# Attention and a SwiGLU block on one Trainium2 core: batch 3's keys turned by transposing transfers, K and V loaded in spread blocks, Q in halves

## The chip, the cores and the metric

The kernel runs on one core of a Trainium2 chip. The core has TensorE (PE, the matmuls; PEld is its weight load), VectorE (DVE), ScalarE (ACT), GpSimd (POOL) and SyncE (SP), each with an instruction queue of its own that is worked off in order, and 16 DMA engines that serve transfers issued from SP, ACT and POOL. The metric is the device time of one execution in microseconds, as a median over runs. Lower is better.

## The reference

Eight batches of causal attention with a learned decay, eight heads of 64, 576 positions, then an RMS norm and a SwiGLU feed-forward over all 4608 tokens. Everything is float32 in HBM.

```python
B, H, S, D = 8, 8, 576, 64
cum    = np.cumsum(np.maximum(s, 0.0), axis=-1)
scores = q @ k.T / 8 + np.minimum(-(cum_q - cum_k), 0.0)     # causal: k <= q
attn   = softmax(scores) @ v                                  # per batch and head
x      = attn as [4608, 512]
xn     = x / sqrt(mean(x * x) + 1e-6) * rms_g
out    = (silu(xn @ w_gate) * (xn @ w_val)) @ w_out           # 512 -> 1536 -> 512
```

Keys further back than the block before a query's own are left out, with a check at the end that what they weigh is negligible.

## The kernel before

**Chunks and slots.** The feed-forward runs over nine chunks of 512 tokens (`ffn`, lines 741 to 781). A chunk is 144 matmuls of 128x512: twelve times four for the gate (L751), twelve times four for the value (L760), and four times twelve for the output (L773). After each group of four the function `step` (L676) is called once. So a chunk has 36 *slots*, and slot 36c belongs to the end of chunk c's predecessor. Attention of the batches to come is laid into these slots: in each slot `step` takes at most one item from each of several lists, and `place` (L712) puts one piece of attention on PE. Nothing of this is decided on the chip: the Python program works through the slots once, with the planner's lags in slots, and writes every engine's instructions in that order. `done` holds the slot in which a piece was placed, and `ready(lag, key)` says whether it lies `lag` slots back. On the chip semaphores keep the data right; a lag only decides how much time lies between a transfer's issue and its reader.

**A batch's way.** Q, K and V of a batch are cut into five blocks of 128 rows (the last has 64).
- Q comes as float32 by one transfer of 1 MB from ACT's queue (`loads`, L486: `load_kq`, then `load_kq_tail`, three slots apart at least), is cast to bfloat16 into `kqn` by POOL in five pieces (`cast_x`), and from batch 2 on is turned into `kqT` by five transposing transfers from SP's queue (`kq_dma`, L170).
- K of batches 0 to 3 (`b < KB`, KB = 4) comes and is cast in the same way, and is turned on PE: four `t_step` (four transposing matmuls each into PSUM, and a copy to `kqT` by ACT, L203) and one `tail_step` (L220, copy L227). `t_seq` is the list of these. K of batches 4 to 7 comes by five casting transfers from POOL's queue straight into `kqn` (`load_k`, L162) and is turned by `kq_dma` as well. The five `load_k` stand at the head of POOL's list `pool_side`, one in each even slot.
- V comes by five casting transfers from POOL's queue (`load_v`, L186), from the list `v_side`, one in each odd slot.
- `s_step` (L278) makes the scores of a block of keys and half of the heads; ACT makes exponentials of them (L302) out of one PSUM buffer `psS`, POOL masks them (L311), and five slots or more later `av_step` (L344, L350) multiplies by V. Then come the norm (ACT L366, POOL L379 and L382, DVE L389) and `xt_dma` (L394), a transposing transfer from SP that writes `xnT`, which the chunk reads.

`can_s` (L619) decides when scores may stand: for batch 2 and on, five slots after the transfer of Q's block and the one after it, and for `b >= KB` five slots after K's block too. SP's queue holds, in the order of the slots, `kq_dma`, `xt_dma` and the stores of the output.

`free(w)` in `casts` (L519) lets a batch's half of `kqn` be written once the batch two before has been checked by DVE (`check_mag`, L420) and turned. `phase()` is the slot within the chunk.

Of the kernel before, what the change touches and what calls it, by code (L numbers as in the profile page):

```python
# [26 lines left out]
def kernel(  # L27
# [12 lines left out]
    nc = tc.nc  # L40
# [40 lines left out]
    kqTn = kqT.rearrange("d a w (h n) -> d a w h n", h=HP)  # L81
    kqTx = kqT.rearrange("d a w (c h n) -> d a w c h n", c=NSC, h=HP)
    XB = 2
    KB = 4
    v_sb = mp.tile([128, 2, NSC, H, NV], BF16, name="v_sb")

    NE = 8
# [39 lines left out]
    def load_kq(eng, b, w, h0=0, h1=H):  # L127
        src = k if w == 0 else q
        eng.dma_start(
            out=kq32[:, w, h0:h1, 0:256],  # L130
            in_=src[b, h0:h1, 0:512, :].rearrange("h (p r) d -> p h (r d)", r=4))
# [299 lines left out]

    SLOTS = 36
    K2 = 34
    slot = [0]
    first, chunk = [0], [0]
    done = {}
    last = {"S": -9, "AV": -9, "T": -9, "X": -9, "AVT": -9, "L": -9}
    s_seq = [(b, kb, g) for b in range(B) for kb in range(NSC) for g in (0, 1) if kb < 4 or g == 0]
    s_seq.sort(key=lambda x: (1, 0, x[2], x[1]) if x[0] == 1 and x[1] < 2 else (x[0], x[1], x[2], 0))
    av_seq = [(b, qb, g) for b in range(B) for qb in range(NSC) for g in (0, 1)]  # L440
# [3 lines left out]
    t_seq.sort(key=lambda x: (x[0], 9, 0, 0) if x[1] == "tail" else  # L444
               (x[0], x[1] // 2, x[2], x[1]) if x[0] == 1 else (x[0], x[2], x[1], 0))
    pending = []
    pool_side, dve_side, v_side, act_side = [], [], [], []
    x_seq = []

    def at(*key):  # L450
# [2 lines left out]
    def ready(lag, *key):  # L453
        return at(*key) + lag <= slot[0]
# [30 lines left out]

    def loads(b, w, when, lag):  # L486

        def main():
            load_kq(nc.scalar, b, w)
            last["L"] = slot[0]  # L490

        def tail():
            load_kq_tail(nc.scalar, b, w)
            done["raw", b, w] = last["L"] = slot[0]
        n = len(act_side)
        when(act_side, lag, [main, tail])
        act_side[n:] = [(lambda c=c: c() and slot[0] - last["L"] >= 3, f) for c, f in act_side[n:]]

    def casts(b):

        def key(c):
            load_k(b, c)
            done["K", b, c] = slot[0]
            if c == NSC - 1:
                check(b)

        def over(w):
            done["cast", b, w] = slot[0]  # L510
            if b + 1 < B and (w == 1 or b + 1 < KB):
                loads(b + 1, w, early, 4)
            if w == 1:
                x_seq.extend((b, ww, c) for c in range(NSC) for ww in ((1, 0) if b >= KB else (1,)))
            else:
                done["cast", b] = slot[0]
                check(b)

        def free(w):  # L519
            return ready(0, "check", b - 2, w) and (  # L520
                ready(0, "T", b - 2) if w == 0 and b < KB + 2 else
                b < XB + 2 or ready(4, "X", b - 2, w, 4))
        if b >= KB:
            pool_side.extend((lambda: free(0) and slot[0] % 2 == 0, lambda c=c: key(c)) for c in range(NSC))
        fns = [(1, lambda r=r: cast_x(nc.gpsimd, b, 1, r)) for r in range(NSC)]
        if b == 2:
            fns[-1] = (1, lambda: (cast_x(nc.gpsimd, b, 1, NSC - 1), over(1)))
        else:
            fns += [(1, lambda: over(1))]
        if b < KB:  # L530
            fns += [(0, lambda r=r: cast(nc.gpsimd, b, 0, r, r + 1)) for r in range(NSC)]
            fns += [(0, lambda: over(0))]
        if b == 2:

            def put2(queue, *fs):
                queue.extend((lambda: slot[0] >= K2 and free(0) and free(1), f) for f in fs)
            put2(act_side, *[lambda r=r: cast_x(nc.scalar, b, 1, r) for r in (3, 4)],
                 *[lambda r=r: cast(nc.scalar, b, 0, r, r + 1) for r in (0, 1, 2)])
            put2(pool_side, *[lambda r=r: cast_x(nc.gpsimd, b, 1, r) for r in (0, 1)],
                 lambda: (cast_x(nc.gpsimd, b, 1, 2), over(1)),  # L540
                 lambda: cast(nc.gpsimd, b, 0, 3, 4), lambda: (cast(nc.gpsimd, b, 0, 4, 5), over(0)))
            return
        pool_side.extend((lambda w=w: ready(7, "raw", b, w) and free(w), f) for w, f in fns)
# [5 lines left out]
    def after_av(b):  # L549
        if b + 2 < B:  # L550
            if b == 0:
                v_side.extend((lambda: chunk[0] == 1, f) for f in (
                    lambda: (load_v(2, 0), load_v(2, 1)), lambda: (load_v(2, 2), load_v(2, 3)),
                    lambda: (load_v(2, 4), done.__setitem__(("V", 2), slot[0]))))
                return
            early(v_side, 6, [lambda r=r: load_v(b + 2, r) for r in range(NSC)]
                  + [lambda: done.__setitem__(("V", b + 2), slot[0])])

    def do_t(key, **kw):
        b, hp, w = key  # L560
# [58 lines left out]
    def can_s():  # L619
# [6 lines left out]
        if slot[0] - last["S"] < (4 if slot[0] < due - 24 else 3 if slot[0] < due else 2):  # L626
            return False
        if b >= XB:
            return all(ready(5, "X", b, 1, c) for c in (kb, min(kb + 1, 4))) and (
                ready(5, "X", b, 0, kb) if b >= KB else ready(3, "T", b) if kb >= 3 else  # L630
                all(ready(3, "T", b, hp, 0) for hp in (2 * g, 2 * g + 1)))
        if kb >= 3 and not ready(3, "T", b):
            return False
# [4 lines left out]
    def can_av(clear=False):  # L638
# [4 lines left out]
            return False  # L643
        if b > 0 and g == 1 and slot[0] - last["T"] < 3 and not clear:
            return False
        if b > 1 and not ready(8, "V", b):
            return False
        if qb > 0 and not ready(5, "S", b, qb - 1, g):
            return False
# [26 lines left out]
    def step(bare=False):  # L676
# [28 lines left out]
        if slot[0] % 2 and not bare and not (chunk[0] == 0 and phase() >= 24):  # L705
            run_side(v_side)
        if not bare:
            run_side(pool_side)
        place()
        run_side(dve_side)  # L710
# [525 lines left out]
```

## Time and profile before

| | |
|---|---|
| device time, three runs | 363.77, 365.58, 370.51 us; median 365.58 |
| profiled execution: device time | 364.69 us |
| its span | 363.0 us |
| granted TensorE clock | 0.999 |
| feed-forward matmuls L751, L760, L773 | 432 of each, 111.1, 111.1 and 102.5 us busy |
| scores L278, AV L344 and L350 | 320, 256 and 320 matmuls |
| exponentials L302 on ACT | 328, 107.0 us busy |
| transposing transfers | 50 for `kqT`, 36 for `xnT` |
| bytes read from HBM, written | 37.90 MB, 9.44 MB |

Chunk 0's first matmul (L751) begins at 26.8 us, chunk 8's last (L773) at 356.5. The attention of batch 0 stands ahead of chunk 0; batch 3's lies in chunks 1 to 3, batch 7's scores end in chunk 6. A row of groups has line, engine, operation, tiles and shapes, count, then busy time, mean nanoseconds of one, the idle time before it and what ended that. A row of waits has who waited, for whom, the total in us, the number of times and the longest.

### The profile page before, as it was taken

What the parts mean: (1) busy time and instruction counts of PE and PEld (TensorE: products, weight loads), DVE (VectorE), ACT (ScalarE), POOL (GpSimd) and SP (SyncE); (2) the same over time, 40 slices, a digit from 0 to 9 for tenths busy, and PEclk for the clock granted to TensorE, in tenths of its full rate; (3) what the DMA queues carried; (4) which work ended last, traced back from release to release, by engine and by line L of the source; (5) the groups of instructions that cost most, each with busy time, mean ns of one, the idle gap of its engine ahead of it and who ended that gap; (6) DMA issues with size and microseconds to landing.
All of it is one profiled execution on the core that took longest, in us unless ns stands there. A gap on an engine that the chain in (4) does not pass through costs nothing. (4 is left out here: it accounts for less than half of the span.)

```text
span 363.0 us, 6976 instructions
## 1 busy us (share of the span) xinstructions
PE 348.8 (96%) x2383; PEld 160.5 (44%) x2383; DVE 273.4 (75%) x523; ACT 239.8 (66%) x619; POOL 178.2 (49%) x283
## 2 busy tenths in 40 slices
PE   4989999999999999999999999999999999999993
PEld 2445444444445444444444444444444444444441
DVE  6697988698888889788998988884588548827820
ACT  3988884768886778877778768776777653223311
POOL 7959765858865566869737954622232200000000
PEclk9999999999999999999999999999999999999999
DMA  7999999999969399969979994973201130020011
GB/s 228 132 229 256 177 170 259 182 201 193 212 127 138 59 198 138 167 147 163 164 202 124 140 142 105 115 85 90 78 14 17 51 103 1 0 88 29 1 60 60
DMA packets 124096, 45.81 MB, mean 126 GB/s; under 512 B 103956, under 2 KB 118808, under 8 KB 124056
## 3 DMA queue, kind: packets, MB, share of 16 engines
q0 software_dynamic: 62688, 14.29, 47.4%
q1 hardware_dynamic: 51872, 23.80, 32.1%
q10 hardware_dynamic: 9496, 7.23, 8.4%
q8 instruction: 19, 0.31, 0.4%
q14 instruction: 21, 0.17, 0.2%
HBM read 37.90 MB, written 9.44 MB: 130 GB/s over the span
## 5 line engine op out<-in xcount | busy, mean ns | idle before, releaser
L302 ACT ACTIVATE E<-psS,biasK 128x256 bf16<-128x256 f32 (+3 forms) x328 | 107.0, 415 | 18.9 <-PE psS L278 18.6
L751 PE MATMUL psF<-xnT,wg_sb 128*128 128x512 bf16 x432 | 111.1, 379 | 0.6 <-ACT xnT L416 0.3
L760 PE MATMUL psF<-xnT,wv_sb 128*128 128x512 bf16 x432 | 111.1, 379 | 0.0
L773 PE MATMUL psF<-wout_sb,Ht 128*128 128x512 bf16 x432 | 102.5, 379 | 0.1
L763 DVE SCALAR_TENSOR_TENSOR U<-T,psF 128x512 bf16<-128x512 f32 x108 | 73.7, 682 | 29.4 <-ACT T L754 29.4
L754 ACT ACTIVATE T<-psF 128x512 f32<-128x512 f32 x108 | 64.4, 596 | 41.0 <-PE psF L751 38.6
L311 POOL TENSOR_SCALAR_AFFINE_SELECT E<-E 128x512 bf16<-128x512 bf16 x64 | 46.5, 727 | 77.5 <-ACT E L302 77.0
L756 DVE TENSOR_TENSOR Ht<-U,psF 128x512 bf16<-128x512 bf16 x99 | 67.7, 684 | 7.0 <-PE psF L760 0.5
L751 PEld LDWEIGHTS <-wg_sb 128*128 128x128 bf16 x432 | 38.7, 98 | 44.9 <-issue 5.6
L773 PEld LDWEIGHTS <-Ht 128*128 128x128 bf16 x432 | 38.6, 97 | 42.4 <-issue 2.3
L760 PEld LDWEIGHTS <-wv_sb 128*128 128x128 bf16 x432 | 38.5, 98 | 42.2 <-issue 4.2
L778 ACT ACTIVATE osb<-psF 128x512 f32<-128x512 f32 x36 | 21.5, 596 | 32.0 <-PE psF L773 25.5
L389 DVE SCALAR_TENSOR_TENSOR xs_sb<-x_sb,al_all,g_row 128x512 bf16<-128x512 bf16 (+1 forms) x36 | 29.9, 831 | 12.8 <-POOL al_all L382 12.1
L186 POOL DMA_DIRECT2D v_sb<-in_v_dram x40 | 35.4, 888 | 0.7 <-PE psAV L350 0.3
L366 ACT ACTIVATE xs_sb<-x_sb 128x512 bf16<-128x512 bf16 (+1 forms) x37 | 23.5, 636 | 17.9 <-DVE x_sb L359 17.5
L427 DVE TENSOR_TENSOR acc<-acc,mag 128x1280 bf16<-128x1280 bf16 x32 | 26.6, 845 | 0.2
L278 PE MATMUL psS<-kqT 64*128 64x256 bf16 (+2 forms) x304 | 25.9, 256 | 0.9 <-ACT kqT L203 0.5
L350 PEld LDWEIGHTS <-E 128*128 128x128 bf16 x320 | 21.7, 98 | 10.0 <-issue 0.2
L379 POOL TENSOR_SCALAR al_all<-ss_all 128x1 f32<-128x1 f32 (+2 forms) x39 | 10.7, 274 | 29.7 <-ACT xs_sb L366 22.9
L382 POOL TENSOR_TENSOR al_all<-al_all,mhalf 128x1 f32<-128x1 f32 (+2 forms) x39 | 22.2, 570 | 3.2
L344 PEld LDWEIGHTS <-E 128*128 128x128 bf16 x256 | 20.0, 98 | 8.6 <-DVE x_sb L359 1.6
L278 PEld LDWEIGHTS <-kqT 64*128 64x128 bf16 x320 | 9.2, 94 | 30.8 <-issue 29.9
(126 smaller groups left out, 301.0 us busy)
## 6 DMA issues: line engine op xcount, KB each, us to landing
out_dram<-osb SPq DMA_DIRECT2D x36, 256.0 KB, 2.3
kq<-in_q_dram ACTq DMA_DIRECT2D x5, 1024.0 KB, 6.2
v_sb<-in_v_dram POOLq DMA_DIRECT2D x32, 128.0 KB, 6.4
kq<-in_k_dram SPq DMA_DIRECT2D x4, 512.0 KB, 5.6
kq<-in_q_dram SPq DMA_DIRECT2D x4, 512.0 KB, 7.5
kqn<-in_k_dram POOLq DMA_DIRECT2D x16, 128.0 KB, 5.4
wout_sb<-in_moe_w_out_dram POOLq DMA_DIRECT2D x2, 768.0 KB, 9.9
kq<-in_q_dram POOLq DMA_DIRECT2D x1, 1024.0 KB, 10.8
```

The lines of the kernel that those rows point to most:

```text
L186: nc.gpsimd.dma_start(out=v_sb[0:n, b % 2, c, :, 0:64], in_=v[b, :, c * 128:c * 128 + n, :].rearrange("h p d -> p h d"))
L278: nc.tensor.matmul(pair[par][:, j * W:j * W + M], lhsT=kT, rhs=qT, start=(j == 0 and not premask), stop=(j == nj - 1))
L302: nc.scalar.activation(out=eo, in_=ei, func=AF.Exp, scale=0.125, bias=biasK[:, kb, bh:bh + 1])
L311: nc.gpsimd.affine_select(out=Ev[:, :, 0:nq], in_=Ev[:, :, 0:nq], pattern=[[0, nh], [1, nq]], compare_op=ALU.is_ge, fill=0.0, base=0, chan ...
L389: nc.vector.scalar_tensor_tensor(out=xs_sb[0:n, (b * NSC + qb) % NX, :], in0=x_sb[0:n, (b * NSC + qb) % NX, :], scalar=al_all[0:n, col:col ...
L427: nc.vector.tensor_tensor(out=acc[:, sl], in0=acc[:, sl], in1=mag[:, sl], op=ALU.max)
L751: nc.tensor.matmul(Gp, lhsT=wg_sb[:, cc, fs], rhs=xnT[:, cc, x0:x0 + DM], start=(cc == 0), stop=(cc == CC - 1))
L754: nc.scalar.activation(out=T, in_=Gp, func=AF.Tanh, scale=0.5)
L756: nc.vector.tensor_tensor(out=Ht[:, fb - 1, :], in0=pend[0], in1=pend[1], op=ALU.mult)
L760: nc.tensor.matmul(Vp, lhsT=wv_sb[:, cc, fs], rhs=xnT[:, cc, x0:x0 + DM], start=(cc == 0), stop=(cc == CC - 1))
L763: nc.vector.scalar_tensor_tensor(out=U, in0=T, scalar=1.0, in1=Gp, op0=ALU.add, op1=ALU.mult)
L773: nc.tensor.matmul(Op, lhsT=Ht[:, fb, tb * 128:(tb + 1) * 128], rhs=wout_sb[:, fb, :], start=(fb == 0), stop=(fb == FB - 1))
```

## The change

- `KB` is 3 instead of 4. Batch 3's K goes the way that batches 4 to 7's went: five `load_k` from POOL and five `kq_dma` from SP in place of the ACT load, the five casts on POOL, four `t_step` and the `tail_step` on PE. Its scores read `kqT` in the layout by blocks.
- K's blocks stand in a list of their own, `k_side`, which `step` serves ahead of `pool_side` in the same slot, in even slots, at least `SPREAD` = 4 slots apart.
- V's blocks for batches 4 to 7 keep 4 slots apart, batch 3's two; batch 2's come at slots 37, 43 and 47 instead of 37, 39 and 41. `can_av` asks for the block `("V", b, qb)` instead of the whole batch.
- From batch 4 on Q's main load is two transfers of four heads each, three slots apart at least.
- Scores of batches 3 to 7 stand at least seven slots, instead of five, behind the transfers that turn their blocks.

The planner's order follows from these. As the program is written, batch 3's scores start at slots 75, 78, 82, 85, 89, 91, 96, 100 and 103 (before: 73, 86, 89, 91, 93, 95, 99, 102 and 105).

```diff
-    KB = 4
+    KB = 3
...
+    SPREAD = 4
...
-    pool_side, dve_side, v_side, act_side = [], [], [], []
+    pool_side, k_side, dve_side, v_side, act_side = [], [], [], [], []
...
     def loads(b, w, when, lag):
-        def main():
-            load_kq(nc.scalar, b, w)
+        def main(h0=0, h1=H):
+            load_kq(nc.scalar, b, w, h0, h1)
             last["L"] = slot[0]
...
-        when(act_side, lag, [main, tail])
+        when(act_side, lag, [main, tail] if b < KB + 1 else [lambda: main(0, 4), lambda: main(4, 8), tail])
...
         def key(c):
             load_k(b, c)
+            last["K"] = slot[0]
             done["K", b, c] = slot[0]
...
-        if b >= KB:
-            pool_side.extend((lambda: free(0) and slot[0] % 2 == 0, lambda c=c: key(c)) for c in range(NSC))
+        keys = [(lambda: free(0) and slot[0] % 2 == 0 and slot[0] - last["K"] >= SPREAD, lambda c=c: key(c))
+                for c in range(NSC)] if b >= KB else []
+        k_side.extend(keys)
...
     def after_av(b):
         if b + 2 < B:
             if b == 0:
-                v_side.extend((lambda: chunk[0] == 1, f) for f in (
-                    lambda: (load_v(2, 0), load_v(2, 1)), lambda: (load_v(2, 2), load_v(2, 3)),
-                    lambda: (load_v(2, 4), done.__setitem__(("V", 2), slot[0]))))
+                def block(*rs):
+                    for r in rs:
+                        load_v(2, r)
+                        done["V", 2, r] = last["V"] = slot[0]
+                v_side.extend((lambda t=t: slot[0] >= SLOTS + t, lambda rs=rs: block(*rs))
+                              for t, rs in ((1, (0, 1)), (7, (2, 3)), (11, (4,))))
                 return
-            early(v_side, 6, [lambda r=r: load_v(b + 2, r) for r in range(NSC)]
-                  + [lambda: done.__setitem__(("V", b + 2), slot[0])])
+            t0 = slot[0] + 6
+
+            def block(r):
+                load_v(b + 2, r)
+                done["V", b + 2, r] = last["V"] = slot[0]
+            v_side.extend((lambda: slot[0] >= t0 and phase() < 24 and slot[0] - last["V"] >= (SPREAD if b > 1 else 2),
+                           lambda r=r: block(r)) for r in range(NSC))
...
         if b >= XB:
-            return all(ready(5, "X", b, 1, c) for c in (kb, min(kb + 1, 4))) and (
-                ready(5, "X", b, 0, kb) if b >= KB else ready(3, "T", b) if kb >= 3 else
+            lag = 7 if b >= KB else 5
+            return all(ready(lag, "X", b, 1, c) for c in (kb, min(kb + 1, 4))) and (
+                ready(lag, "X", b, 0, kb) if b >= KB else ready(3, "T", b) if kb >= 3 else
...
-        if b > 1 and not ready(8, "V", b):
+        if b > 1 and not ready(8, "V", b, qb):
...
         if not bare:
+            run_side(k_side)
             run_side(pool_side)
```

2 lines of the change are left out of this document (1 added, 1 removed).

## The prediction

> **What bounds the kernel now.** I read the page first, its busy shares and its forty slices, for the engine that has no room.
>
> ```profile
> PE 348.8 (96%) x2383; PEld 160.5 (44%) x2383; DVE 273.4 (75%) x523; ACT 239.8 (66%) x619; POOL 178.2 (49%) x283
> PE   4989999999999999999999999999999999999993
> PEclk9999999999999999999999999999999999999999
> ```
>
> TensorE is busy in 96% of the span, nine tenths or more of every slice after the fourth, at the full granted clock. The second view is the table of waits, cut to 62 to 183 us, where all that the change moves takes place. These are all waits of PE in it:
>
> ```profile
> PE psS L278 <- ACT E L302: 0.3, 2, 0.2
> PE psF L751 <- DVE rZ L357: 0.2, 1, 0.2
> ```
>
> Half a microsecond in 121. So the stage is a row of matmuls without holes: only fewer matmuls make it shorter, and any wait makes it longer by its whole length. How fast the transfers are counts only where one is later than the matmul that reads it. The third view is the timeline of PE around two of the steps that go, and at the first matmuls of chunks 2 and 3.
>
> ```profile
> 100.85 1.04 PE L773 MATMUL psF<-wout_sb,Ht 128*128 128x512 bf16 x4
> 101.72 0.39 PE L195 MATMUL psT<-ident_bf,kqn 128*128 128x128 bf16 x4
> 101.94 0.38 PE L773 MATMUL psF<-wout_sb,Ht 128*128 128x512 bf16 x1
> ...
> 120.01 0.39 PE L220 MATMUL psT<-ident_bf,kqn 128*128 128x128 bf16 x4
> 120.23 1.03 PE L760 MATMUL psF<-xnT,wv_sb 128*128 128x512 bf16 x4
> ...
> 107.06 0.38 PE L751 MATMUL psF<-xnT,wg_sb 128*128 128x512 bf16 x1
> ...
> 145.95 0.39 PE L751 MATMUL psF<-xnT,wg_sb 128*128 128x512 bf16 x1
> ```
>
> Matmuls overlap, so their price is read from start to start, not from the second column. Chunk 2 takes 145.95 - 107.06 = 38.9 us for 36 slots: a slot is 1.08 us. Slot 72 is the 107.06.
>
> **What goes from PE.** Batch 3's keys cost four t_steps and a tail_step. Four transposing matmuls of a t_step take 101.94 - 101.72 = 0.22 us, the four of the tail 120.23 - 120.01 = 0.22 us. Five steps make 1.10 us, and it all lies on the path, since PE has nothing to wait for there. No matmul is added: the changed program has twenty weight loads and twenty matmuls fewer on PE and no warming matmul more. **-1.10 us.**
>
> **What goes from and comes to ScalarE and GpSimd.**
>
> ```profile
> L203 ACT ACTIVATE kqT<-psT 128x512 bf16<-128x512 bf16 x12 | 7.4, 613 | 1.3 <-PE psT L195 1.2
> L227 ACT ACTIVATE kqT<-psT 128x256 bf16<-128x256 bf16 x3 | 1.2, 385 | 0.1
> L129 ACTq DMA_DIRECT2D kq<-in_q_dram x5: 374/393/433, 71.5 to 184.8; - x5
> L156 POOL CAST kqn<-kq 128x512 bf16<-128x512 f32 x23 | 14.6, 656 | 0.0
> L162 POOL DMA_DIRECT2D kqn<-in_k_dram x20: 685/893/1317, 107.2 to 204.2; - x20
> L186 POOL DMA_DIRECT2D v_sb<-in_v_dram x40: 685/891/1311, 9.3 to 234.4; - x40
> L311 POOL TENSOR_SCALAR_AFFINE_SELECT E<-E x29: 624/640/1331, 65.3 to 182.7; 128x512 bf16<-128x512 bf16 x29
> 131.56 0.39 PE L278 MATMUL psS<-kqT 64*128 64x256 bf16 x4 [0.17 <-ACT E L302]
> 161.00:172.00 11.00, 11.00 (x78) 4.94 (x78) 9.70 (x20) 8.15 (x25) 10.38 (x16) 1.00 2.04 194
> ```
>
> ScalarE loses 4 x 0.613 + 0.385 = 2.84 us of copies and two issues of batch 3's K; it gains four issues of 0.39 us for Q's second halves, one for each of batches 4 to 7, which its 66% hide (1.6 us if they didn't). ScalarE is on the path only where two score steps stand two slots apart and the exponentials of the first aren't done. Of the waits above, the 0.17 at 131.56 belongs to S(3,2,1), which stands two slots behind S(3,2,0); in the new order batch 3 has one such pair instead of four steps in a row (slots 89, 91, 93, 95 become 82, 85, 89, 91). I take **-0.17**; nothing at the one end, the 0.3 of both waits at the other.
>
> GpSimd exchanges batch 3's five casts of K, 5 x 0.656 = 3.3 us (at most: the last is half as large), for five issues of 5 x 0.893 = 4.5 us: +1.2 us on an engine at 49%. But the new list lets one slot hold a K issue and a cast together, and V moves into the same place: slots 49 to 57 now hold five issues of V, two of K, batch 3's five casts of Q and four masks, 4.5 + 1.8 + 3.3 + 2.6 = 12.2 us in 9 x 1.08 = 9.7. It falls 2.5 us behind there and catches up after. In the stretch 161 to 172, the last of the rows, GpSimd was busy 10.38 of 11.00 us and PE all 11.00. So I take **0**; the price of the uncovered case is in the rivals. K's first block waits for VectorE's check of batch 1's keys, whose read of kqn stands at slot 45, seven slots ahead: nothing.
>
> **What comes to SyncE and the DMA engines.** Five transposes of K join ten that a batch of the later kind has already.
>
> ```profile
> L182 SPq DMA_TRANSPOSE kqT<-kqn x50: 1186/1232/1921, 69.1 to 247.8; - x50
> 103.90 1.19 SPq L400 DMA_TRANSPOSE xnT<-xs_sb  x1
> 105.18 1.23 SPq L182 DMA_TRANSPOSE kqT<-kqn  x1
> ```
>
> Each holds SyncE's queue for 1.23 us, 6.2 us in all. The queue is in order, and what is behind it matters at a chunk's start: xnT of (2,2), at slot 67, must land before 107.06. In both orders one kqT transfer stands between xnT (2,1) and (2,2) (Q's block 1 before, K's block 0 after), so nothing is added there if K's block 0, issued at slot 52 and turned at slot 64, has come: 12 x 1.08 = 13.0 us. Of the issues of K into kqn the slowest needed 8.1 us:
>
> ```profile
> DMA to landing us min/median/max: 3.5/5.4/8.1
> ```
>
> The first of them belongs to slot 70, at 104.9, and went out at 107.2, 2.3 us behind: 2.3 + 8.1 = 10.4, in time. V's issues between 70 and 92 us are nearer to slot 52, and they took longer:
>
> ```profile
> DMA to landing us min/median/max: 6.9/8.2/11.5
> ```
>
> At their slowest K's block would come at 13.8, 0.8 us late, and the 0.8 could reach chunk 2's start; at the median it is 2.5 early. For chunk 3 the block needed, (3,2), moves from slot 103 to 100, three slots safer. **0**, with 0.8 as the upper end.
>
> **The new wait: scores seven slots behind the turned Q.** This is what decides. By the planner's slots batch 3's S(kb,0) and the Q block that it needs last stand as follows: before, S at 73, 89, 93, 99, from 9 to 27 slots behind; after, S at 75, 82, 89, 96, each exactly 7 behind. Batch 4 went 17, 14, 15, 13; it goes 7, 7, 8, 9. From batch 5 on it is 10 or more. So eight score steps lose their reserve. From batch 3 on V's blocks are loaded 28 slots or more before their use in both, and K's turned blocks stand 9 or more ahead.
>
> The room is 7 x 1.08 = 7.56 us. Of it goes what SyncE lags: Q's block (3,1,2) belongs to slot 68, four slots ahead of 107.06, so at 102.7; its issue is the 105.18 above, 2.4 us later. About 5.2 us are left for the landing. The landings of kqT, four windows of the view by tile (the whole run; issues from 98 to 160; from 158 to 176; from 69 to 91):
>
> ```profile
> DMA to landing us min/median/max: 2.3/4.7/11.4
> DMA to landing us min/median/max: 2.3/4.6/7.4
> DMA to landing us min/median/max: 6.5/6.7/8.0
> DMA to landing us min/median/max: 5.4/9.1/11.4
> ```
>
> The steps concerned lie between 110 and 162 us, so the second row is nearest: at its median none of the eight waits, at its maximum each waits 7.4 - 5.2 = 2.2 us. Nothing can come out below zero here, for no matmul is taken away. I take two of eight late by 0.4 us, near the median end, because K and V come spread and the loads' bursts get shorter: **+0.8**, with ends 0 and 8 x 2.2 = 17.6.
>
> **The sum.** The profiled execution took 364.69 us (span 363.0 and 1.7 around it): 364.69 - 1.10 - 0.17 + 0 + 0 + 0.8 = **364.2 us**. The median shown, 365.58, is 0.9 above the profiled one, and the three runs lie 6.7 us apart, so 2% is about what a measurement of this kernel can tell from no change. The forecast is inside it.
>
> **The rivals.**
>
> *Nothing waits.* The landings stay at 4.6 us or less: 364.69 - 1.10 - 0.3 = 363.3 us. For it speaks the row of waits, in which no DMA holds back a score; against it that those scores had 9 to 27 slots of reserve. Chance 0.23.
>
> *The transposes land late* (the other side). K, V, Q's halves and both kinds of transposes now run together from 84 to 160 us. Where that was so before, from 158 to 176, landing took 6.7 us; it was 3.8 where less ran:
>
> ```profile
> 98.00:113.00 15.00, 15.00 (x118) 7.32 (x117) 11.66 (x22) 12.27 (x40) 9.21 (x14) 1.00 0.93 157
> 158.00:176.00 18.00, 18.00 (x130) 8.12 (x128) 15.55 (x29) 12.66 (x38) 15.87 (x25) 1.00 1.86 166
> DMA to landing us min/median/max: 2.7/3.8/5.5
> ```
>
> The next to last figure is the DMA share: 0.93 and 1.86. (The last row is kqT from 98 to 118.) With 6.7 us each of the eight waits 6.7 - 5.2 = 1.5, and 8 x 1.5 = 12 goes to PE unless SyncE uses the pauses to run ahead; with a quarter won back so, 9 us: 364.69 - 1.27 + 9 = 372.4 us. It decides from a mean wait of (7.3 + 1.27) / 8 = 1.07 us on, where the 2% lie; under that it ends between 366 and 372. Against it: the change takes the bursts apart. Chance 0.32, of which 0.20 beyond 2%. The Trainium skill ("DMA: Bandwidth & Descriptors", section "Issuing engines are not separate DMA queues") says that transfers started by any engine run on the same 16 DMA engines and interleave, so the blocks that GpSimd issues would hold up SyncE's transposes; by that rule the time would be the 372.4, and the two windows here agree with it, 3.8 us at a share of 0.93 and 6.7 us at 1.86. The same page ("Rules for kernel authors") wants transfers of 1 MiB or more, against which K in blocks and Q in halves go; the next two rows agree, since an eighth of the bytes lands hardly sooner.
>
> ```profile
> kq<-in_q_dram ACTq DMA_DIRECT2D x5, 1024.0 KB, 6.2
> kqn<-in_k_dram POOLq DMA_DIRECT2D x16, 128.0 KB, 5.4
> ```
>
> *GpSimd comes late with a mask.* AV follows its scores by five slots, 5.4 us, and the mask stands between. With GpSimd 2.5 us behind in slots 49 to 57, and again where casts, K and V meet in batches 4 and 5 (slots 83 to 88, 116 to 120), a mask can be a microsecond late: +1 to +6 in all, 365 to 369 us. Against it the full stretch 161 to 172 without a wait of PE. Chance 0.12, 0.02 of it beyond 2%.
>
> **How the numbers follow.** The forecast (363.7 to 365.7) has 0.33, the three rivals 0.23, 0.32 and 0.12. To be over 2% faster it would have to be under 357.4, and all that can go from PE is 1.4 us: 0.02, for a disturbed comparison. Slower by over 2%: 0.20 + 0.02, and 0.02 for a wait that I don't see: 0.24. Within 2%: 0.74. The range begins at 362.4, a microsecond under the case without waits for the scatter of runs, and ends at 372.0, at the 2%, short of the worse half of the second rival.
>
> **What would show it.** PE has 2363 matmuls instead of 2383; L195 on psT counts 16 fewer, L220 four fewer, L203 four fewer on ScalarE; L162 counts 25 and L182 55. Chunk 2, 38.9 us now, becomes about half a microsecond shorter if nothing waits. A new row of waits of PE or its weight loads at L278 for kqT's transfer, at batches 3 and 4, is the second rival; a wait at L344 or L350 for E's mask is the third. I am wrong if PE waits more than 3 us between 84 and 183 us, or if the gain is over 2 us.

## The result, and the profile after

| | before | after |
|---|---|---|
| device time, median of four runs each on one chip | 366.37 us (363.77 to 370.51) | 371.57 us (370.97 to 373.32) |
| profiled execution: device time, span | 364.69, 363.0 us | 372.14, 370.5 us |

The ratio is 1.0164, with a 95% interval from 1.0128 to 1.0200: slower, by 6 us, clear of the noise, and still inside the 2%. (The ratio leaves out the slow run of 370.51 us, so it stands against a median of 365.58.) The forecast was 364.2 us, half a microsecond faster than the profiled run before, so its sign was wrong. The time lies in the range, but at its upper end, near the price of the second rival.

The page of the changed kernel, its busy shares, PE's forty slices and the granted clock in each:

```profile
PE 350.0 (94%) x2363; PEld 159.9 (43%) x2363; DVE 273.1 (74%) x523; ACT 237.4 (64%) x614; POOL 181.8 (49%) x283
PE   5989999899989997989999999999999999999993
PEclk9999999999999999999999999999999999999998
```

The 20 matmuls are gone and the clock is full, but the row of nines has holes. A slice is 9.26 us. The 8 in slices 8, 12 and 18 and the 7 in slice 16 (which is 139 to 148 us) have no counterpart in the row before. The waits of PE between 62 and 183 us, where the kernel before had 0.5 us in all, name them (who waited for whom, total us, times, longest):

```profile
PE psS L278 <- DMA kqT<-kqn: 3.6, 2, 2.0
PE psF L764 <- DMA xnT<-xs_sb: 1.9, 2, 1.5
PE psS L278 <- ACT E L302: 0.8, 2, 0.6
PE psF L764 <- DVE U L776: 0.3, 1, 0.3
PE psAV L350 <- POOL E L311: 0.2, 1, 0.2
```

(The feed-forward's lines have moved by 13: gate L764, value L773, output L786.) The first row is new and the largest: two scores that waited for a turned block. The timeline of PE at both (start, length, instruction, in brackets the idle time before it):

```profile
144.08 0.29 PE L278 MATMUL psS<-kqT 64*128 64x64 bf16 x8 [1.98 <-DMA kqT<-kqn]
...
159.07 0.39 PE L278 MATMUL psS<-kqT 64*128 64x256 bf16 x4 [1.65 <-DMA kqT<-kqn]
```

The view by tile, of `kqT` on SyncE, in two short windows, gives the issue (count, nanoseconds, when) and what it took to land.

```profile
L182 SPq DMA_TRANSPOSE kqT<-kqn x1: 1260/1260/1260, 135.2 to 135.2; - x1
DMA to landing us min/median/max: 8.8/8.8/8.8
...
L182 SPq DMA_TRANSPOSE kqT<-kqn x1: 1331/1331/1331, 152.0 to 152.0; - x1
DMA to landing us min/median/max: 7.0/7.0/7.0
```

135.2 + 8.8 is 144.0, and 152.0 + 7.0 is 159.0: PE went on within 0.1 us of each landing. The first, an S of 64 keys and 64 queries, is S(3,4,0), the scores of batch 3's last block of keys; the block that came last is K's last one, of 64 rows, nine slots ahead of it. The second is S(4,1,0), seven slots behind Q's block.

Where the rest went is read from the first gate matmul of each chunk (us; the last line is the changed kernel with a lag of ten, an experiment below):

| chunk | 1 | 2 | 3 | 4 | 5 | 6 |
|---|---|---|---|---|---|---|
| before | 68.41 | 107.06 | 145.95 | 183.68 | 221.11 | 258.16 |
| after | 69.41 | 109.61 | 149.12 | 189.07 | 228.65 | 265.84 |
| after less before | 1.00 | 2.55 | 3.17 | 5.39 | 7.54 | 7.68 |
| lag of ten | 68.98 | 108.92 | 146.35 | 184.22 | 224.16 | 261.34 |

From chunk 6 on the difference stands still; the change is felt from 68 to 229 us only. Of the 7.68 us, 1.00 is there when chunk 1 begins, with a wait for a turned x. Before slot 39 both programs have the same order, so the change's order can't have made it. The new order also moves whole pieces of attention from one chunk to the next, so the difference of a chunk isn't made by waits alone. Chunk 1 itself loses 1.55 us, with waits for x, E and a mask. Chunk 2 loses 0.62, though PE has 16 matmuls fewer in it, 12 of them transposing: the wait for kqT is longer than what these give back. Chunk 3 loses 2.22, of which the second wait for kqT is 1.7. Chunk 4 loses 2.15, of which the view names 0.7 us of PE's waits, for VectorE's U and ScalarE's E; the rest it doesn't name.

### The profile page after: what moved, and what is told of

Its sections match the earlier page's. It is cut to its first block, busy times and chain, and to the rows that moved or that the text cites. A ratio compares the mean times of both kernels' runs of the same rounds, so it can differ in the third digit from the quotient of the medians.

```text
span 370.5 us, 6952 instructions
## 1 busy us (share of the span) xinstructions
PE 350.0 (94%) x2363; PEld 159.9 (43%) x2363; DVE 273.1 (74%) x523; ACT 237.4 (64%) x614; POOL 181.8 (49%) x283
## 5 line engine op out<-in xcount | busy, mean ns | idle before, releaser
L764 PE MATMUL psF<-xnT,wg_sb 128*128 128x512 bf16 x432 | 111.0, 379 | 3.0 <-DMA xnT<-xs_sb 1.9
L773 PE MATMUL psF<-xnT,wv_sb 128*128 128x512 bf16 x432 | 111.1, 380 | 0.0
L786 PE MATMUL psF<-wout_sb,Ht 128*128 128x512 bf16 x432 | 101.9, 379 | 0.1
L776 DVE SCALAR_TENSOR_TENSOR U<-T,psF 128x512 bf16<-128x512 f32 x108 | 73.7, 682 | 33.8 <-ACT T L767 33.8
L764 PEld LDWEIGHTS <-wg_sb 128*128 128x128 bf16 x432 | 39.1, 98 | 48.1 <-issue 7.4
L786 PEld LDWEIGHTS <-Ht 128*128 128x128 bf16 x432 | 38.9, 98 | 43.7 <-issue 2.3
L773 PEld LDWEIGHTS <-wv_sb 128*128 128x128 bf16 x432 | 38.4, 98 | 42.9 <-issue 5.0
L389 DVE SCALAR_TENSOR_TENSOR xs_sb<-x_sb,al_all,g_row 128x512 bf16<-128x512 bf16 (+1 forms) x36 | 28.8, 799 | 15.1 <-POOL al_all L382 14.3
L427 DVE TENSOR_TENSOR acc<-acc,mag 128x1280 bf16<-128x1280 bf16 x32 | 27.6, 879 | 0.4
L162 POOL DMA_DIRECT2D kqn<-in_k_dram x25 | 24.3, 970 | 0.2 <-issue 0.2
```

What stands on the lines that cost most here:

```text
L389: nc.vector.scalar_tensor_tensor(out=xs_sb[0:n, (b * NSC + qb) % NX, :], in0=x_sb[0:n, (b * NSC + qb) % NX, :], scalar=al_all[0:n, col:col ...
L427: nc.vector.tensor_tensor(out=acc[:, sl], in0=acc[:, sl], in1=mag[:, sl], op=ALU.max)
L764: nc.tensor.matmul(Gp, lhsT=wg_sb[:, cc, fs], rhs=xnT[:, cc, x0:x0 + DM], start=(cc == 0), stop=(cc == CC - 1))
L773: nc.tensor.matmul(Vp, lhsT=wv_sb[:, cc, fs], rhs=xnT[:, cc, x0:x0 + DM], start=(cc == 0), stop=(cc == CC - 1))
L776: nc.vector.scalar_tensor_tensor(out=U, in0=T, scalar=1.0, in1=Gp, op0=ALU.add, op1=ALU.mult)
L786: nc.tensor.matmul(Op, lhsT=Ht[:, fb, tb * 128:(tb + 1) * 128], rhs=wout_sb[:, fb, :], start=(fb == 0), stop=(fb == FB - 1))
```

## The experiments

The ratio of each run is against runs of the kernel before on the same chip. Two causes were put against each other: *turned blocks land too late for the seven slots*, and *GpSimd is late* (with masks, with the norm's factor, with casts).

**1. Lag of twelve.** The changed kernel with

```diff
-            lag = 7 if b >= KB else 5
+            lag = 12 if b >= KB else 5
```

> The changed kernel with one number changed: scores of batches 3 to 7 stand twelve slots behind the turned blocks instead of seven (batch 3's start at slot 80 instead of 75, the others move by 1 to 5 slots). In the changed kernel PE waits 3.8 us for kqT's transfers (144.08 and 159.07 us) and some 3 us more in pieces that follow GpSimd. Theory 1 (the reserve behind the transposes is what is missing): both waits for kqT go, the time falls by 3 to 4.5 us against the changed kernel, to a ratio of 1.004 to 1.009 to the kernel before. Theory 2 (GpSimd is late and drags masks, norms and ScalarE with it): the pieces stay, the time falls by under 1.5 us, ratio 1.012 or more. Chunk 3's x has one slot less of reserve than before the change (5), which could cost up to 1 us.

368.50 us, ratio 1.0037 (1.0006 to 1.0069). No wait for kqT is left in its profile. PE's waits between 62 and 215 us:

```profile
PE psF L764 <- DMA xnT<-xs_sb: 2.2, 2, 1.5
PE psS L278 <- ACT E L302: 1.1, 3, 0.6
PE psT L344 <- DVE x_sb L359: 0.4, 1, 0.4
PE psAV L350 <- POOL E L311: 0.2, 1, 0.2
```

One edit, which touches no engine's work, takes 1.27 of the 1.64%, some 4.6 us, as the first theory said. The 1.5 us for xnT is at chunk 3's start, where the turned x of batch 3 now has five slots instead of nine.

**2. K and the rest never in one slot.**

```diff
-            run_side(k_side)
-            run_side(pool_side)
+            if not run_side(k_side):
+                run_side(pool_side)
```

> The changed kernel, but in a slot in which a block of K is issued nothing is taken from GpSimd's other list, so that a K issue and a cast no longer share a slot. The scores of batches 3 and 4 keep their slots (seven behind the turned blocks). Theory 1: PE's waits for kqT stay, the gain is under 1.5 us, ratio 1.012 to 1.020. Theory 2: the pieces of waiting from 165 to 217 us (2.9 us at first matmuls on L764 and at the masks) go, and with them 2.5 to 3.5 us: ratio 1.007 to 1.010.

375.69 us, ratio 1.0236 (1.0156 to 1.0316), longer than either theory had it. PE's small waits for U and E between 165 and 217 us went from 1.0 us to nothing, with 0.2 for Ht in their place; but the two lists now stretch each other, the reserves of batches 5 and 6 shrink to seven slots as well, and PE waits for kqT three times, 7.4 us in all against 3.6 in the changed kernel. The transposes took back more than GpSimd won.

**3. KB = 4, all else as changed.** Batch 3's keys go back to PE; Q's halves begin at batch 4 as in the change.

```diff
-    KB = 3
+    KB = 4
...
-        when(act_side, lag, [main, tail] if b < KB + 1 else [lambda: main(0, 4), lambda: main(4, 8), tail])
+        when(act_side, lag, [main, tail] if b < 4 else [lambda: main(0, 4), lambda: main(4, 8), tail])
```

> The changed kernel with batch 3's keys turned on PE again (KB = 4; Q in halves from batch 4 on, spread K and V and the lag of seven stay). PE gets its twenty transposing matmuls back, +1.1 us. Scores of batch 3 stand 9 to 33 slots behind Q's transposes, batch 4's ten or more. Theory 1: no wait for kqT, ratio 1.002 to 1.008. Theory 2: the spread lists alone make GpSimd late (by the slots its backlog in chunk 1 is as long as in the changed kernel), so 2 us or more of pieces stay: ratio 1.008 to 1.014. If the ratio is 1.000 within its interval, the five blocks of batch 3's K are the whole cause.

370.37 us, ratio 1.0096 (1.0058 to 1.0133). The waits for kqT fall to 0.5 us, and still 3.5 us are lost: the new lists and the halves cost time without one more key being turned by a transfer.

**4. The kernel before, once more.**

> The kernel before once more, for its profile. Up to slot 36 the two kernels are written alike, yet the changed one waited 1.6 us at chunk 1's first matmul for xnT of block (1,2) and the one before 0.4. If that is chance, this profile shows a wait of another length there (0.3 to 2 us), and elsewhere between 72 and 250 us none over 0.4 us. If it is the change's doing, it shows 0.4 again.

367.4 us. PE's wait for x at chunk 1's start is 0.2 us here, 1.5 in the changed kernel: it comes and goes without the change. Against the expectation this execution has a wait of 1.2 us for kqT:

```profile
87.17 0.39 PE L278 MATMUL psS<-kqT 64*128 64x256 bf16 x4 [1.20 <-DMA kqT<-kqn]
```

It is S(2,1,0). Q's block stands eleven slots ahead of it; it was issued at 76.5 and took 10.5 us to land. Batch 2's first score, the only one seven slots behind, didn't wait. So a reserve of eleven slots can fail too, and what is new with the change is how many scores stand at seven to nine.

**5. Only KB = 3.** The kernel before with one figure changed:

```diff
-    KB = 4
+    KB = 3
```

> The kernel before with one figure changed, KB = 3 in place of 4: batch 3's keys are turned by the transfers, and nothing else is as in the change. K's blocks stand in GpSimd's old list again, V is loaded together, Q whole, and scores may run five slots behind a turned block. Scores of batches 3 and 4 then stand 5 to 13 slots behind their last block (7 to 18 in the changed kernel), and GpSimd is never more than 1.6 us behind its slots (up to 3.3 in the changed kernel). If transposes that land late are the loss: PE waits for kqT in batches 3 and 4 for 5 us or more in all (3.8 in the changed kernel), and the ratio to the kernel before is 1.012 to 1.04. If GpSimd that comes late is the loss: the small waits for mask, U and x_sb stay as in the kernel before, PE waits for kqT no more than the 3.8 us, and the ratio is 0.997 to 1.008.

381.33 us, ratio 1.0408 (1.0330 to 1.0487), the longest time of all, though by the planner's slots GpSimd is less behind here than in the changed kernel. PE's row of waits for kqT, and its longest wait in the timeline:

```profile
PE psS L278 <- DMA kqT<-kqn: 10.9, 6, 6.5
```

```profile
122.74 0.61 PE L278 MATMUL psS<-kqT 64*128 64x256 bf16 x4 [6.47 <-DMA kqT<-kqn]
```

That block was issued at 114.3 and landed 8.3 us later, at 122.6. This speaks for the transposes: GpSimd works off the old kind of lists, and the time is longer, not shorter. Lags of five slots (with the old lists), seven, ten and twelve give 1.041, 1.016, 1.007 and 1.004; the last two agree by their intervals.

**6. Lag of ten**, and **8.** the same with **Q loaded whole** (`[main, tail]` for every batch).

```diff
-            lag = 7 if b >= KB else 5
+            lag = 10 if b >= KB else 5
```

> The changed kernel with scores ten slots behind a turned block in place of seven. Every score of batches 3 and 4 then stands ten slots or more behind its last block, and the turned x of batch 3 gets seven slots ahead of its FFN (nine in the changed kernel, five with a lag of twelve). If late transposes are the main loss: no wait for kqT above 0.6 us, the 1.71 us wait for xnT that a lag of twelve showed at 149 us is gone or below 0.6, and the ratio to the kernel before is 1.000 to 1.005. If a margin of ten is not enough: one or two waits of 1 to 2 us for kqT, ratio 1.006 to 1.012. GpSimd's lists are those of the changed kernel, so a GpSimd theory that leaves nothing to the transposes says 1.012 to 1.02.

> The changed kernel with scores ten slots behind a turned block and Q loaded whole, as in the kernel before (main and tail, no halves). Reserves as in the run with a lag of ten; GpSimd's largest lag behind its slots between 84 and 168 falls from 2.4 to 2.0 us, and ScalarE issues ten transfers fewer. If the halves cost time (ScalarE's own issues before its E, or smaller packets): 0.3 to 1 us below the run with a lag of ten, ratio 0.996 to 1.003. If they cost nothing: the same as that run to 0.3 us. If halves are needed so that a block of Q lands sooner: waits for kqT of 1 us or more come back, ratio 1.006 or above.

367.85 us, ratio 1.0072 (1.0041 to 1.0104), and 368.62 us, 1.0047 (1.0014 to 1.0079): one result, by their intervals. Neither profile has a wait for kqT; that the halves buy or cost anything beyond the noise isn't shown (Q whole saves four transfers, not the ten of the expectation). The table of chunks shows what remains with a lag of ten. Chunk 2 takes 146.35 - 108.92 = 37.43 us, 1.46 less than the 38.89 before. It has 24 matmuls fewer: 12 transposing ones (the other eight of the twenty were in chunk 1), and one group of four scores and one of eight AV matmuls that the new order puts into other chunks. From start to start these take 3 x 0.22, 0.33 and 0.24 us in the kernel before, 1.2 in all. Chunk 4 takes 39.94 us, 2.51 more than the 37.43 before, with 124 matmuls of attention in both. PE's waits from 184 to 215 us name half of it, and VectorE first:

```profile
PE psF L764 <- DVE U L776: 1.1, 3, 0.6
PE psS L278 <- ACT E L302: 0.2, 1, 0.2
```

**7, 9, 10, 11. The other parts.** The third run with V together as before (the excerpt shows its main edit; `can_av` is as before too); then the kernel before with K's own list alone, with Q's halves alone, with V's spread alone.

```diff
-            v_side.extend((lambda: slot[0] >= t0 and phase() < 24 and slot[0] - last["V"] >= (SPREAD if b > 1 else 2),
-                           lambda r=r: block(r)) for r in range(NSC))
+            early(v_side, 6, [lambda r=r: load_v(b + 2, r) for r in range(NSC)]
+                  + [lambda: done.__setitem__(("V", b + 2), slot[0])])
```

> The third run again (the changed kernel with KB = 4, ratio 1.0096), with V's blocks issued as in the kernel before. K's list of its own and Q's halves (from batch 4 on) stay. GpSimd is then at most 2.0 us behind its slots (3.5 us in the third run). If the spread of V, which puts V's issues into GpSimd's busy slots 36 to 60, is what makes GpSimd late there: ratio 0.999 to 1.004, and the waits for U, x_sb and ScalarE's E between 100 and 175 us shrink to the 1.5 us in all of the kernel before. If K's own list or Q's halves are the loss: 1.006 to 1.012.

> The kernel before with one of the four edits: K's blocks in a list of their own, four steps apart, so that a block can share a slot with a cast. KB stays 4, V together, Q whole. Scores of batches 4 to 7 keep 13 slots or more behind their blocks, as in the kernel before; GpSimd's largest lag behind its slots rises from 2.5 to 3.7 us, between slots 120 and 168. If GpSimd that comes late there is the part of the loss that is not late transposes: ratio 1.003 to 1.010, with waits for U, Ht, ScalarE's E or masks of 1.5 us or more in all between 135 and 190 us. If it is not: 0.998 to 1.002.

> The kernel before with one of the four edits: Q's blocks from batch 4 on loaded in halves. KB stays 4, K's blocks stand in GpSimd's old list, V together. The scores of batches 4 to 7 come to ten slots or more behind their blocks (13 in the kernel before), and GpSimd is never more than 2.5 us late, as before. The GpSimd theory and the theory of late transposes both say no change: 0.998 to 1.002. If ScalarE's extra issues are a cost of their own (two starts of 892 ns by the row of the kernel before for each batch): 1.002 to 1.006 and longer waits for E.

> The kernel before with one of the four edits: V's blocks spread. KB stays 4, K's blocks in GpSimd's old list, Q whole. GpSimd's largest lag rises from 2.5 to 3.5 us at slots 60 to 72, and to 1.9 us at 156; reserves as in the kernel before. If the spread of V makes GpSimd late in slots 36 to 72: ratio 1.002 to 1.006, with waits of 1 us or more in all for masks, x_sb or E between 95 and 130 us that the kernel before does not have. If not: 0.998 to 1.002.

368.93 us, 1.0071 (1.0033 to 1.0110); 372.93, 1.0206 (1.0163 to 1.0250); 371.59, 1.0172 (1.0126 to 1.0218); 370.69, 1.0127 (1.0096 to 1.0158). No expectation had this: each part alone has a longer median than three of them together (1.0096), for K's list clear of the intervals. The three ratios would add up to 5%, so a theory that gives each a price of its own is wrong. The profiled executions of K's list and Q's halves took 369.82 and 368.38 us, some 3 us less than their medians, so their profiles show only part of the loss. Two of the four profiles (V together, halves alone) have one wait of 1.6 and 1.8 us at 183 us that the view lays to ScalarE and to nothing. It is a turned block: with V together PE went on at 182.97 (timeline), and the transfer issued at 172.6 took 10.2 us (view by tile), eleven slots of reserve notwithstanding. With halves alone PE went on at 183.13, and the transfer issued at 172.8 took 10.2 us too; it has a second wait for kqT, of 1.2 us, at 79 us in batch 2.

```profile
182.97 0.29 PE L278 MATMUL psS<-kqT 64*128 64x256 bf16 x2 [1.57 <-ACT osb L783]
```

```profile
L182 SPq DMA_TRANSPOSE kqT<-kqn x1: 1708/1708/1708, 172.6 to 172.6; - x1
DMA to landing us min/median/max: 10.2/10.2/10.2
```

The others show the second cause at work, in two forms. With K's list alone, the norm's factor `al_all` stands in GpSimd's queue behind an issue and a cast, VectorE waits 2.28 us for it with U and Ht queued behind, and PE waits for Ht (GpSimd, VectorE and PE in the timeline):

```profile
202.33 0.89 POOL L186 DMA_DIRECT2D v_sb<-in_v_dram  x1
203.22 0.62 POOL L156 CAST kqn<-kq 128x512 bf16<-128x512 f32 x1
203.94 0.19 POOL L379 TENSOR_SCALAR al_all<-ss_all 128x1 f32<-128x1 f32 x1
204.21 0.56 POOL L382 TENSOR_TENSOR al_all<-al_all,mhalf 128x1 f32<-128x1 f32 x1
...
204.81 1.08 DVE L389 SCALAR_TENSOR_TENSOR xs_sb<-x_sb,al_all,g_row 128x512 bf16<-128x512 bf16 x1 [2.28 <-POOL al_all L382]
...
206.53 0.38 PE L765 MATMUL psF<-xnT,wv_sb 128*128 128x512 bf16 x1 [1.77 <-DVE Ht L761]
```

With V's spread alone, the scale of x itself is held. Its median there is 0.75 us; beside GpSimd's casts without a pause it took 2.81:

```profile
156.15 2.81 DVE L389 SCALAR_TENSOR_TENSOR xs_sb<-x_sb,al_all,g_row 64x512 bf16<-64x512 bf16 x1
156.64 1.17 POOL L156 CAST kqn<-kq 128x512 bf16<-128x512 f32 x2
157.76 0.64 POOL L311 TENSOR_SCALAR_AFFINE_SELECT E<-E 128x512 bf16<-128x512 bf16 x1
158.35 1.07 POOL L145 CAST kqn<-kq 128x512 bf16<-128x512 f32 x1
159.42 0.68 DVE L776 SCALAR_TENSOR_TENSOR U<-T,psF 128x512 bf16<-128x512 f32 x1
...
160.15 0.38 PE L764 MATMUL psF<-xnT,wg_sb 128*128 128x512 bf16 x1 [1.50 <-DVE U L776]
```

The scale ended at 158.96, 0.56 us after the mask's end at 158.40, and the cast that follows the mask took 1.07 where its neighbours took 0.59: which reads as VectorE standing first, then GpSimd.

**12. Lag of ten, slots not shared, Q whole**: the two remedies together.

```diff
-        when(act_side, lag, [main, tail] if b < KB + 1 else [lambda: main(0, 4), lambda: main(4, 8), tail])
+        when(act_side, lag, [main, tail])
...
-            lag = 7 if b >= KB else 5
+            lag = 10 if b >= KB else 5
...
-            run_side(k_side)
-            run_side(pool_side)
+            if not run_side(k_side):
+                run_side(pool_side)
```

> The changed kernel with three things mended: scores ten slots behind a turned block, a slot that issues a block of K takes nothing else from GpSimd's other list (as in the second run), and Q whole. Every score of batches 3 to 7 stands ten slots or more behind its block; GpSimd is at most 1.9 us late after slot 72 (3.3 us remain at 48 to 60 from V). If late transposes and GpSimd that comes late together make the whole loss, what is left is the 20 turned groups that PE no longer does (1.1 us) against some 0.5 us at slots 48 to 60: ratio 0.996 to 1.000, faster than the kernel before. If something else costs time: 1.003 to 1.007, as with a lag of ten alone.

369.58 us, ratio 1.0098 (1.0068 to 1.0128): a miss. No wait for kqT, but 2.5 us for U. One of these, 1.6 us, stands behind a scale of x again, which took 2.2 us beside three casts and a mask in a row. That K's issue shares a slot with a cast isn't the matter, then; GpSimd's other work is enough.

**13, 14, 15. Without the masks.** GpSimd's `affine_select` on E is left out (`return` as the first line of `mask`), in the kernel before, with a lag of ten, and in the changed kernel. These three don't compute the reference: scores above the diagonal stay in.

> The kernel before without the causal masks on E (GpSimd's 64 selects of 727 ns in the row of the kernel before; scores above the diagonal are then left in). It is the base of the two runs that follow. Order and all else are the same. In the kernel before GpSimd is rarely late, so both theories expect little: ratio to the kernel before 0.990 to 1.000.

> The sixth run (the changed kernel with a lag of ten) without the causal masks on E. If a late GpSimd makes what is left of the loss: the waits for U, Ht and E between 93 and 110 us and between 189 and 206 us shrink to below 1 us in all (some 3 us there with the masks), and the time is 0.5 to 1.5 us below that of the kernel before without masks, which is what the 20 turned groups are worth. If the order on DVE and ScalarE makes it: the waits stay, and the time is 1.5 to 3 us above that of the kernel before without masks.

> The changed kernel without the causal masks on E. Late transposes do not depend on the masks: 2 to 5 us of waits for kqT stay, and the time is 2 to 5 us above that of the run with a lag of ten without masks. If GpSimd were the cause of those waits too (its casts feed the turned blocks of K): no wait for kqT above 0.5 us, and the time of the two runs is the same to 0.5 us.

367.54 us (365.82 to 369.64), 366.26 us (365.63 to 367.33) and 367.19 us (365.51 to 370.39). PE's waits from 62 to 215 us, first of the kernel before:

```profile
PE psF L752 <- DMA xnT<-xs_sb: 2.8, 2, 1.7
PE psS L278 <- ACT E L302: 0.3, 2, 0.2
```

of the lag of ten:

```profile
PE psF L765 <- DMA xnT<-xs_sb: 1.8, 2, 1.2
PE psS L278 <- ACT E L302: 0.6, 3, 0.3
PE psF L765 <- DVE U L777: 0.2, 1, 0.2
```

and of the changed kernel, the two largest rows:

```profile
PE psS L278 <- DMA kqT<-kqn: 2.5, 2, 1.8
PE psF L765 <- DVE U L777: 0.6, 2, 0.4
```

With a lag of ten the version that turns batch 3 by transfers is no longer behind: 1.3 us below its base, as the GpSimd theory said, though the two ratios to the kernel before (0.9976, 0.9949 to 1.0004, and 1.0024, 0.9986 to 1.0063) overlap. Against its own ratio with masks (1.0072, 1.0041 to 1.0104) the lag of ten gained clear of the intervals, and the kernel before gained nothing (1.0024). The waits for U and E shrank, from 184 to 215 us from 1.3 to 0.4 us, but not to nothing. The waits for kqT stay in the changed kernel, as the transposes' theory said, but its time is only 0.9 us above the lag of ten where 2 to 5 were expected: in the profiled runs 1.8 us of waits for xnT stand on the other side. The two waits for xnT of the kernel before, 2.8 us, show that these come and go without the change. And the changed kernel's ratio fell from 1.0164 to 1.0022 (0.9982 to 1.0062) with its lag of seven left as it was. So a longer lag and a lighter GpSimd each take back most of the loss; the two causes overlap, and their gains can't be added.

**16, 17, 18. Masks on VectorE.** With a lag of ten, the masks of batches 2 to 5 (K's last blocks excepted) multiplied in on VectorE, all or every second one; and every second one in the kernel before. The excerpt is from the first run; the other two add `and g == 1` to the condition. `tri` holds ones and zeros, and the output is whole.

```diff
+            if kb < 4 and 2 <= b <= 5:
+                nc.vector.tensor_tensor(
+                    out=Ev[:, :, 0:nq], in0=Ev[:, :, 0:nq], in1=tri, op=ALU.mult)
+                return
             nc.gpsimd.affine_select(
```

> The sixth run (lag of ten) with the masks of batches 2 to 5 (32 of the 64; K's last blocks excepted) multiplied in on VectorE, by a triangle of ones and zeros that GpSimd makes once; the output is whole. GpSimd loses 32 selects of 727 ns, 23 us. VectorE gains 32 products of 128x512 in bf16; its product of U by the value in the same shape, which reads PSUM, takes some 690 ns, its halves of 128x1280 in the check of K 750 ns, so 0.3 to 0.7 us each, 10 to 22 us on an engine that is busy for 129 of 152 us there. If GpSimd's load is what is left: ratio 0.997 to 1.002, the waits for U and Ht between 189 and 206 us gone. If VectorE's order is as tight: new waits for U and x_sb, 1.006 to 1.02.

> As the run before, with every second mask only (16 masks, those of the second group of heads). GpSimd loses 12 us, VectorE gains 5 to 11 us. If GpSimd's load is what is left: 0.997 to 1.003, and not above the run with all 32 where VectorE is the tighter of the two. If neither helps: 1.004 to 1.008, as with the lag of ten alone.

> The kernel before with every second mask of batches 2 to 5 on VectorE: what the move is worth without the change. GpSimd is rarely late there, so by the theory of a late GpSimd it gives nothing: 0.998 to 1.004. If it is faster by 0.3% or more, the move and not the lag makes the gain in the run before this one.

379.09 us, 1.0352 (1.0290 to 1.0415); 372.62, 1.0185 (1.0113 to 1.0256); 373.56, 1.0196 (1.0120 to 1.0272). The first run's 32 products in the view by tile (min, median, max in ns), and PE's largest row of waits (its gate is L776):

```profile
L320 DVE TENSOR_TENSOR E<-E,tri x32: 410/422/1436, 80.7 to 224.6; 128x512 bf16<-128x512 bf16 x32
```

```profile
PE psF L776 <- DVE U L788: 5.2, 9, 1.1
```

A product takes 0.42 us, 13.5 in all, and the run is some 10 us longer than with a lag of ten: on VectorE, which also makes U and Ht in order, the products hold up PE. The load only changed places, and in the kernel before half of the move costs 1.96% without the change, so these runs can't say what GpSimd's load is worth. No version that computes everything was faster than the kernel before.

## Why the prediction was wrong

- **-1.10 for the transposes on PE: right by the counts.** PE has 2363 matmuls; the groups of transposes have 16 and 4 fewer than before, ScalarE's copies 4 fewer, and K's issues are 25:

```profile
L195 PE MATMUL psT<-ident_bf,kqn 128*128 128x128 bf16 x36 | 3.7, 220 | 0.0
L220 PE MATMUL psT<-ident_bf,kqn 128*128 128x128 bf16 x12 | 1.0, 219 | 0.0
L203 ACT ACTIVATE kqT<-psT 128x512 bf16<-128x512 bf16 x8 | 4.8, 595 | 0.8 <-PE psT L195 0.7
L162 POOL DMA_DIRECT2D kqn<-in_k_dram x25 | 24.3, 970 | 0.2 <-issue 0.2
```

 Chunk 2, which was to become half a microsecond shorter without waits, became 1.46 shorter with a lag of ten, where nothing waited for kqT; 0.66 of that are its twelve transposing matmuls, and most of the rest is attention that moved to other chunks. In the changed kernel it grew to 39.51, with the first wait for kqT in it.
- **-0.17 for ScalarE: wrong in sign, and small.** The waits for E between 62 and 183 us rose from 0.3 to 0.8 us.
- **0 for SyncE and xnT: right for chunk 3**, which has no such wait in the changed kernel. The 1.5 us at chunk 1 come ahead of the first slot in which the orders differ; the 0.4 at chunk 2, inside the 0.8 of the upper end, stay open.
- **+0.8 for scores seven slots behind the turned blocks: the step that failed, by its size.** Two scores were forecast late, and two were; 0.4 us each was forecast, and 2.0 and 1.7 were measured. With E, x, U and a mask PE waited 5.3 us between 84 and 183 us, past the 3 that the prediction had named as its sign of being wrong. The typical landing was right, 4.6 forecast, and so nearly was the range up to 7.4; the tile's view from 98 to 160 us after:

```profile
DMA to landing us min/median/max: 2.4/4.7/8.8
```

 The error was to take the value near the median. With ten blocks to a batch the slowest decides, and PE pays whatever it lacks: the two came in 8.8 and 7.0 us. That the forecast had just two late scores is in part luck, for the count looked at Q alone: one of the two was K's last block, put aside with "nine or more ahead". By the lags the whole step is worth 3.4 us (1.0164 against 1.0072) to 4.6 (against 1.0037); the runs without masks show that part of this goes through GpSimd as well, so only the 3.6 us of waits are read directly. That is the second rival's mechanism at a third to a half of its 9 us: it made all eight scores late by the median of the crowded window, 6.7 us, where two were late by the tail.
- **0 for GpSimd: wrong, by 1.4 to 2.6 us over the kernel before** (1.0037 and 1.0072), or a microsecond more if the 1.10 is counted as won. The busy stretch of 161 to 172 us without a wait of PE was no proof of cover: what PE waits for is the norm's factor and the scale of x, and in the profiles they are hit where they fall behind a run of issues and casts. The lag of ten without masks shows that this part goes through GpSimd's work; that its whole size does, the overlap of the two intervals leaves open. The third rival had its size (1 to 6 us) and named the mask; in the changed kernel the mask itself held PE for 0.2 us.

The Trainium skill ("SBUF — State Buffer", section "Who interferes with whom") says that a VectorE instruction with two inputs in SBUF contends with a GpSimd instruction that reads SBUF, since its second input comes through the read interface that the two share. The scale of x has two such inputs, and the 2.81 us beside casts agree with it. In the changed kernel's own profile the longest scale took 1.17 us, so there this form of the cause is small; VectorE's waits for the norm's factor rose from 12.1 us in all to 14.3.

Not settled: why K's list, Q's halves and V's spread cost 1.3 to 2.1% each alone and 1.0% together. Both causes occur in their profiles, in other places each time; which part moves which wait wasn't tried further. Each run left one profile, so how often a block lands as late as the ones shown isn't known.

## What to carry to other kernels

Where one engine is a row without holes, price a transfer's reserve by its slowest landings under the load of its new place, not by the median, and count every block that a reader needs. A lag that costs little to lengthen should be varied first: one figure gave back between half and three quarters of this loss. And where several in-order engines are fitted closely to each other, try each part of a change alone as well, since here the parts didn't add up.

## What was not expected of the hardware

A transposing transfer of the same 128 KB landed in 2.4 us (the changed kernel, issued at 144.9) or in 13.7 (the kernel before once more, issued at 77.9), and the slowest of the changed kernel between 98 and 160 us, 8.8, was one of half that size. The load beside it differed: from 135 to 144 us, in the 8.8 us transfer's time, the DMA share was 1.67, with blocks of V and K and half of a Q in flight; from 145 to 147.4 us it was 0.73. VectorE's scale of x, 0.75 us as a rule, took up to 3.6 us beside GpSimd's casts (V spread alone, at 177 us). In the three cases of over 2 us that were followed (2.2, 2.8 and 3.6 us), casts and masks stood in GpSimd's queue without a pause between them.
